# Dilated attention and a squared-ReLU FFN on one core: two more batches take the quadrant form of attention

## The chip, the cores and the metric

The kernel runs on one core of a Trainium2 chip. The metric is device time in microseconds: 310.31 us before, the median of three runs (309.73 to 311.42).

## The reference

Eight batches of eight heads, 576 tokens, head size 64. Heads 0 to 3 attend to the last 32 tokens (plain), heads 4 to 7 to every fourth of the last 128 (dilated). The attention output of all batches, 4608 tokens of 512 features, goes through a feed-forward network (FFN) with a squared ReLU.

```python
scores = scale * np.matmul(q, k.transpose(0, 1, 3, 2))
rel = pos[:, None] - pos[None, :]
mask_plain = (rel >= 0) & (rel < window)                              # window = 32
mask_dil = (rel >= 0) & (rel < window * dilation) & (rel % dilation == 0)   # dilation = 4
attn = np.exp(scores - max); attn = attn / np.sum(attn)
out = np.matmul(attn, v)                      # (8, 8, 576, 64)
x = out.transpose(0, 2, 1, 3).reshape(4608, 512)
h = np.maximum(x @ w_in, 0.0)                 # 512 -> 2048
return h * h @ w_out                          # 2048 -> 512
```

## The kernel before

**The order of the work is written by hand.** The FFN is cut into 288 groups, g0 to g287, mostly of four matmuls of 512 columns: for a tile of 512 tokens 16 groups of the first layer (L880, `mm1`, each followed by a ReLU on ACT, L893, and a square on DVE, L894) and 16 of the second (L922, `g2`; every fourth is followed by a copy to `osb` on ACT and a store). The first two tiles are done in halves of 256 tokens, 16 groups each (g0 to g63); g64 begins the tile of tokens 1024 to 1535, g96 the next. Each tile needs the attention output `xT` of its tokens: g48 to g51 those of batch 1's end, g64 to g67 those of batch 2, g96 those of batches 2 and 3. In g48 to g51 and g64 to g67 the first three heads' features come first (`cut = 3`) and the fourth head's two groups later. Attention is put between the groups: `PROGRAM` lists, divided by `|`, the steps that follow each group, and a list `steps` adds those of the quadrant form at a group number. Every engine carries out its instructions in the order in which they are issued here, and waits at the first one whose inputs or buffers aren't ready.

**PSUM.** Four buffers `pf` (FFN accumulators; also the spare pair of a step with an `f`), two `pa`, one `po`, one `pd`.

**The old form** (batches 1 to 3; batch 0 has one of its own). Heads go in pairs e = 0 to 3 (0, 1 plain, 2, 3 dilated; order 0, 2, 1, 3). Steps of `PROGRAM`, as `2k0` = batch 2, step k, pair 0: `q`, `k` make the transposed queries and keys, by transposes on TensorE (`trans`, L241) or from the crossbar buffer `xx` that a transposing DMA filled (`cross`), and copy them with `halves` (L261 to L278) into `qT` and `kbd`, where keys stand block by block, the two heads of a pair on the diagonal of a 128x128 block, zeros beside them. `v` spreads values likewise (`spread_v`, L212). `a`, `b` compute the scores of a pair's first and second half (`scores`, L317, L323, then Exp on ACT, L327, and the mask on DVE, L328; batch 3 also adds overlapping columns into `pm`, L337). `o`, `p` multiply by the values and sum (`pv`, L427, L429), take the reciprocal by Ln and Exp (L431, L432) and write `xT` (L442). A half is one step, so the eight halves of a batch take turns on two `pa` buffers.

**The quadrant form** (batches 4 to 7; `NATURAL = 4`). Queries and keys of all heads come from `xx` (for batch 2, XB, only the dilated heads are crossed; `xx[b % 2]` is the buffer). `arrange`: K, eight DVE copies of the plain heads' keys (L499), Q, four (L496), R, four small ones for the dilated heads' remainders (L504, L507). Then `quadrants` issues matmuls on 64x64 quarters of the array: S the scores of a pair into a pair of `pa` tiles, B first the values and sums of the pair before (into `po`, `pd` and the last 64 columns of the new `pa` tiles) and then the scores of the next, P values alone. E0 and E1 are Exp (L656) and mask (L658) of the two `pa` tiles; L four logarithms (L637, L638), X the exponential (L642) and three products into `xT` (L645, L647). A bundle B takes both `pa`, `po` and `pd`, so it needs E of its own scores and X of the values before. Bundles stand eight groups apart, L at the group of the bundle, X one later, E two and three later.

**Loads.** POOL issues the loads of q, k and v in the order of `PROGRAM`; v for the old form goes by `load_v` into blocks, for the quadrant form by `load_v_rows` into rows. SP issues the stores and the transposing DMAs.

Of the kernel before, what the change touches and what calls it, by code (L numbers as in the profile page):

```python
# [12 lines left out]
RES = 4  # L13
# [14 lines left out]
    "1o0 1o1f | 1a3 1Q0 | 1K0 1o3 | 1Q1 1K1 | 1Q2 | 1b0 | | 1Q3 1K2 L2:vwpdr L3:q00123 L3:q10123 | L2:x | | 2q0 | "  # L28
    "| 2k0 1V2 | 1b2 1p0 | 1b1 1V3 1K3 | | 1p2 1p1f | 2a0 1b3 | 2k1l 2b0 2o0 1p3f 2k1h | 2q1 2k2 L3:x | | 2q2 2p0 "
    "L3:vwpdr 2a1 | | | 2b1 | 2o1 2a2 2v2 2q3 | | 2p1f | 2k3 | 2b2 2o2 | 2v3 | 2a3 2p2f L4:q10123 | 2b3 2o3 | 3k1 "  # L30
    "| 2p3 | 3q1v L4:q00123 | 3k0l | | 3a1 3k0h | | 3k2l | 3o1 3q0a | 3k2h | | | 3a0 | 3b1 | 3q2 | | 3p1 L4:x "
    "L4:V | 3v2 | 3b0 | 3a2 3q3l 3o0 3q3h 3k3 | | | 3o2 3b2 | | 3p0 3v3 | 3a3 | 3p2 | L5:q10123 3b3 | 3o3 | | | "
    "L5:q00123 3p3 L5:V | | | | | | | | | | | | L5:x | | | | L6:q00123 | | | | | | | | | | | | | L6:q10123"
# [28 lines left out]
def kernel(  # L62
# [33 lines left out]
    ADDED = 3  # L96
    NATURAL = 4
# [7 lines left out]
    pm_pool = ctx.enter_context(tc.tile_pool(name="pm", bufs=4))  # L105
# [120 lines left out]
    def trans(b: int, e: int, nm: str, part: int, home: str):  # L226
# [4 lines left out]
        copy = copier(nm, e, home, True)  # L231
        if b == 2:
            m0, n, pitch, cuts = 0, M, M, [(t[0:80, a, :, :], MS[a], 80) for a in range(2)]
        else:

            m0, n, pitch, cuts = MS[part], MN[part], 80, [(t[0:80, part, :, :], 0, 80)]
# [7 lines left out]
        ready[b, e, nm] = pv_[:, :, :, 0:n], m0, n, copy  # L244
        halves(e, nm, *ready[b, e, nm], (0,) if "l" in home else (0, 1))
# [3 lines left out]
    def copier(nm: str, e: int, home: str, early: bool):  # L249
        act = "a" in home or "v" not in home and nm == "q" and e < NE // 2 and early  # L250
        return nc.scalar.copy if act else nc.vector.tensor_copy
# [31 lines left out]
    def blocks(b: int, e: int, part: int):  # L283

        if e < NE // 2:
            if b >= ADDED:
                return [(i, None, 16 * i, min(16 * i + 24, M)) for i in (range(4, NB) if part else range(4))]
            if part == 0:  # L290
                return [(i, None, 16 * i, min(16 * i + 24, 64)) for i in range(4)]
            return [(3, None, 64, 72)] + [(i, None, 16 * i, min(16 * i + 24, M)) for i in range(4, NB)]
        if b not in PARTED:
            rs = (2 * part, 2 * part + 1)
            return [x for r in rs for x in ((r, r, 0, 96), (4 + r, r, 64, M))] + [(8, None, 128, M)] * (part == 0)
        if part == 0:
            return [(r, r, 0, 64) for r in range(RES)]
        return [x for r in range(RES) for x in ((r, r, 64, 96), (4 + r, r, 64, M))] + [(8, None, 128, M)]

    def half_at(b: int, e: int):  # L300

        if e < NE // 2:
            return (384, mask_p[:, 384:832]) if b >= ADDED else (352, mask_p)
        return (256, mask_d) if b in PARTED else (416, mask_h)

    pts, pms = {}, {}

    def scores(b: int, e: int, part: int):
# [5 lines left out]
        for i, r, m0, m1 in blocks(b, e, part):  # L314
# [10 lines left out]
        off, mask = half_at(b, e)  # L325
# [4 lines left out]
            in1=mask[:, off : off + n] if b < ADDED and mask is not mask_h else mask[:, 0:n], op=ALU.mult,  # L330
        )
        if b < ADDED:
            return
        pm = pms[e, part] = pm_pool.tile([P, 160], bf16, name="pm")

        def add(to, x, y):
            nc.vector.tensor_tensor(out=to, in0=x, in1=y, op=ALU.add)  # L337

        if e >= NE // 2:
            main = pt[:, off : off + 352].rearrange("p (r c) -> p r c", r=2)  # L340
            add(pm[:, 0:64].rearrange("p (r m) -> p r m", r=2), main[:, :, 64:96], main[:, :, 96:128])
            return
        i0, n = (3, 4) if part else (0, 3)
        v = pt[:, 96 * i0 : 96 * (i0 + n + 1)].rearrange("p (i r m) -> p i r m", r=RES, m=24)
        add(
            pm[:, 0 : 32 * n].rearrange("p (i r m) -> p i r m", r=RES, m=8),
            v[:, 0:n, :, 16:24], v[:, 1 : n + 1, :, 0:8],
        )
        if part:
            add(  # L350
                pm[:, 128:160].rearrange("p (r m) -> p r m", r=RES), v[:, n, :, 16:24],
                pt[:, 768:832].rearrange("p (r m) -> p r m", r=RES)[:, :, 0:8],
            )

    def pv(b: int, e: int, part: int, spare=None, name=""):
# [8 lines left out]
        c = half_at(b, e)[0] * part  # L364
        byr = dil and b not in PARTED
        mms, dms = [], []
        if byr:
            n = 2 * M
            o3 = o[:, 0:n].rearrange("p (r m) -> p r m", r=2)
            d3 = d[:, 0:n].rearrange("p (r m) -> p r m", r=2)  # L370
            main = pt[:, c : c + 352].rearrange("p (r c) -> p r c", r=2)
            rem = pt[:, 352 + 32 * part : 384 + 32 * part].rearrange("p (r m) -> p r m", r=2)
            for x in range(2):
                mms.append((o3[:, x, 0:96], 2 * part + x, main[:, x, 0:96]))
                mms.append((o3[:, x, 64:M], 4 + 2 * part + x, main[:, x, 96:176]))
            mms.append((o3[:, :, 128:M], 8, rem))
            if b >= ADDED:
                pm = pms[e, part][:, 0:64].rearrange("p (r m) -> p r m", r=2)
                dms += [(d3[:, :, 0:64], main[:, :, 0:64]), (d3[:, :, 64:96], pm), (d3[:, :, 96:M], main[:, :, 128:176])]
            else:  # L380
                dms += [(d3[:, :, 0:96], main[:, :, 0:96]), (d3[:, :, 64:M], main[:, :, 96:176])]
            dms.append((d3[:, :, 128:M], rem))
        else:
            n = RES * MN[part]
            o3 = o[:, 0:n].rearrange("p (r m) -> p r m", r=RES)
            d3 = d[:, 0:n].rearrange("p (r m) -> p r m", r=RES)
            if not dil and b >= ADDED:

                i0 = 4 * part
                p4 = pt[:, 96 * i0 : 96 * i0 + 384].rearrange("p (i r m) -> p r i m", r=RES, m=24)  # L390
                d4 = d3.rearrange("p r (i m) -> p r i m", m=16)
                pm = pms[e, part]
                if part == 0:
                    dms.append((d4[:, :, 1:4, 8:16], p4[:, :, 1:4, 8:16]))
                    dms.append((d4[:, :, 1:4, 0:8], pm[:, 0:96].rearrange("p (i r m) -> p r i m", r=RES, m=8)))
                    dms.append((d4[:, :, 0, :], p4[:, :, 0, 0:16]))
                else:
                    dms.append((d4[:, :, 0:4, 8:16], p4[:, :, :, 8:16]))
                    b3 = pt[:, 288:384].rearrange("p (r m) -> p r m", r=RES)
                    b8 = pt[:, 768:832].rearrange("p (r m) -> p r m", r=RES)  # L400
                    dms.append((d4[:, :, :, 0:8], pm[:, 0:160].rearrange("p (i r m) -> p r i m", r=RES, m=8)))
                    dms.append((d4[:, :, 4, 8:16], b8[:, :, 8:16]))
                    mms.append((o3[:, :, 0:8], 3, b3[:, :, 16:24]))
                    mms.append((o3[:, :, 64:80], 8, b8))
                for i in range(4):
                    m1 = min(16 * i + 24, 64) if part == 0 else 16 * i + 24
                    mms.append((o3[:, :, 16 * i : m1], i0 + i, p4[:, :, i, 0 : m1 - 16 * i]))
            elif dil and part == 0:
                dms.append((d[:, 0:n], pt[:, 0:n]))
            elif dil:  # L410
                main = pt[:, c : c + 448].rearrange("p (r c) -> p r c", r=RES)
                rem = pt[:, c + 448 : c + 512].rearrange("p (r m) -> p r m", r=RES)
                dms += [(d3, main[:, :, 32:112]), (d3[:, :, 0:32], main[:, :, 0:32]), (d3[:, :, 64:80], rem)]
            for i, r, m0, m1 in () if mms else blocks(b, e, part):
                x0, x1 = m0 - MS[part], m1 - MS[part]
                if r is None:
                    w = RES * (m1 - m0)
                    rh = pt[:, c : c + w].rearrange("p (r m) -> p r m", r=RES)
                    mms.append((o3[:, :, x0:x1], i, rh))
                    if not dil:  # L420
                        dms.append((d3[:, :, x0:x1], rh))
                else:
                    w = m1 - m0
                    mms.append((o3[:, r, x0:x1], i, pt[:, c : c + w]))
                c += w
# [7 lines left out]
        t0 = b * S % RING  # L433
        tok = xT[:, e, t0 : t0 + S]
        if byr:
# [678 lines left out]
```

## Time and profile before

| | |
|---|---|
| time, median of three runs | 310.31 us (309.73 to 311.42) |
| profiled execution | 308.71 us, its span 306.8 us |
| TensorE (PE) busy | 295.2 us, 96% of the span, 2870 matmuls in the records |
| VectorE (DVE), ScalarE (ACT), GpSimd (POOL) busy | 177.7, 203.4, 96.1 us |
| granted TensorE clock | 0.999 |
| chain that ended last | PE 86%, DVE 6%, ACT 4% |
| FFN first layer, second layer on PE (L880, L922) | 130.4, 128.6 us busy |
| HBM read, written | 36.90 MB, 9.44 MB |

A group of instructions is named by the line of the kernel that issues it. A timeline's row has start, length, engine, line, operation, output and inputs, shapes, how many instructions were merged (x8), and in brackets the idle time of the engine before it and what ended it. Lengths of merged rows hold one latency at their end, so the pace is taken from starts.

### The profile page before, as it was taken

What the parts mean: (1) busy time and instruction counts of PE and PEld (TensorE: products, weight loads), DVE (VectorE), ACT (ScalarE), POOL (GpSimd) and SP (SyncE); (2) the same over time, 40 slices, a digit from 0 to 9 for tenths busy, and PEclk for the clock granted to TensorE, in tenths of its full rate; (3) what the DMA queues carried; (4) which work ended last, traced back from release to release, by engine and by line L of the source; (5) the groups of instructions that cost most, each with busy time, mean ns of one, the idle gap of its engine ahead of it and who ended that gap; (6) DMA issues with size and microseconds to landing.
All of it is one profiled execution on the core that took longest, in us unless ns stands there. A gap on an engine that the chain in (4) does not pass through costs nothing.

```text
span 306.8 us, 7297 instructions
## 1 busy us (share of the span) xinstructions
PE 295.2 (96%) x2870; PEld 172.3 (56%) x2903; DVE 177.7 (58%) x517; ACT 203.4 (66%) x439; POOL 96.1 (31%) x138
## 2 busy tenths in 40 slices
PE   8899999999999978999999999999999999999995
PEld 3599658769655544554455445544554445445543
DVE  1675567988988995468456855676563234104400
ACT  6888478869869744786579657865786576226511
POOL 8599683893065056230161208000000000000000
PEclk9999999999999999999999999999999999999999
DMA  8999999999979969998299869902200210121022
GB/s 115 196 180 214 204 162 224 174 150 185 154 111 196 157 100 204 139 148 131 69 133 152 103 142 103 164 16 65 61 2 13 68 61 0 35 71 34 0 64 75
DMA packets 80290, 35.09 MB, mean 114 GB/s; under 512 B 49920, under 2 KB 75648, under 8 KB 80256
## 3 DMA queue, kind: packets, MB, share of 16 engines
q0 software_dynamic: 46592, 18.23, 52.6%
q1 hardware_dynamic: 32976, 16.06, 26.0%
q8 instruction: 23, 0.38, 0.5%
q10 hardware_dynamic: 688, 0.33, 0.5%
q14 instruction: 11, 0.09, 0.1%
HBM read 36.90 MB, written 9.44 MB: 151 GB/s over the span
## 4 chain that ended last, share of the span: by engine, by line
PE 86%; DVE 6%; ACT 4%; issue 2%; ACTq 0%
PE pf L922 37%; PE pf L880 36%; PE po L674 2%; PE pa L529 2%; ACT h2T L893 2%; PE pd L529 1%; PE pa L241 1%; DVE h2T L894 1%; PE po L529 1%; PE po L427 1%; PE pa L704 1%; PE pd L429 1%; DVE kbd L499 1%; PE pf L756 1%; PE pa L323 1%
## 5 line engine op out<-in xcount | busy, mean ns | idle before, releaser
L880 PE MATMUL pf<-xT,w_in 128*128 128x512 bf16 (+1 forms) x693 | 130.4, 340 | 0.8
L922 PE MATMUL pf<-w_out_sb,h2T 128*128 128x512 bf16 (+2 forms) x570 | 128.6, 373 | 2.1 <-issue 1.4
L880 PEld LDWEIGHTS <-w_in 128*128 128x128 bf16 x704 | 76.9, 114 | 44.6 <-issue 1.1
L893 ACT ACTIVATE h2T<-pf 128x512 bf16<-128x512 f32 x144 | 82.4, 605 | 17.5 <-PE pf L880 17.0
L894 DVE TENSOR_TENSOR h2T<-h2T 128x512 bf16<-128x512 bf16 x144 | 60.1, 425 | 57.3 <-ACT h2T L893 53.0
L922 PEld LDWEIGHTS <-h2T 128*128 128x128 bf16 x592 | 54.7, 98 | 58.6
L928 ACT COPY osb<-pf 128x512 f32<-128x512 f32 (+1 forms) x36 | 20.7, 576 | 40.5 <-PE pf L922 37.6
L166 POOL DMA_DIRECT2D qb<-in_q_dram x18 | 13.6, 757 | 44.0 <-DMA xx<-qb 32.4
L645 DVE TENSOR_TENSOR xT<-po,rec 128x512 bf16<-128x512 f32 x16 | 11.1, 692 | 23.3 <-ACT rec L642 22.1
L656 ACT ACTIVATE pt<-pa 128x448 bf16<-128x448 f32 (+3 forms) x32 | 16.3, 509 | 9.3 <-DVE xT L647 9.3
L475 POOL DMA_DIRECT2D vd<-in_v_dram x16 | 9.9, 634 | 28.3 <-PE pa L529 24.8
L638 ACT ACTIVATE rec<-pd 64x512 f32<-64x512 f32 x32 | 18.6, 580 | 0.0
L183 POOL DMA_DIRECT2D vbd<-in_v_dram x20 | 13.9, 708 | 8.3 <-DMA kb<-in_k_dram 2.3
L327 ACT ACTIVATE pt<-pa 128x352 bf16<-128x352 f32 (+6 forms) x24 | 11.9, 506 | 4.1 <-PE pa L317 2.9
L431 ACT ACTIVATE rec<-pd 128x256 f32<-128x256 f32 (+2 forms) x19 | 7.8, 410 | 10.1 <-PE pd L429 10.1
L166 POOL DMA_DIRECT2D kb<-in_k_dram x18 | 13.6, 758 | 0.8 <-DMA vbd<-in_v_dram 0.4
L637 ACT ACTIVATE rec<-pa 64x64 f32<-64x64 f32 x32 | 7.0, 219 | 10.1 <-PE pa L529 9.5
L499 DVE COPY kbd<-xx 64x320 bf16<-64x320 bf16 (+1 forms) x32 | 13.0, 508 | 0.4
L484 POOL DMA_DIRECT2D vbd<-in_v_dram x16 | 12.5, 798 | 0.4 <-DMA qb<-in_q_dram 0.4
L442 DVE TENSOR_TENSOR xT<-po,rec 128x256 bf16<-128x256 f32 (+2 forms) x19 | 8.6, 454 | 6.5 <-ACT rec L432 5.7
L432 ACT ACTIVATE rec<-rec 128x256 f32<-128x256 f32 (+2 forms) x24 | 10.6, 443 | 0.8
L642 ACT ACTIVATE rec<-rec 128x576 f32<-128x576 f32 x16 | 10.9, 680 | 0.3
(128 smaller groups left out, 308.2 us busy)
## 6 DMA issues: line engine op xcount, KB each, us to landing
qb<-in_q_dram POOLq DMA_DIRECT2D x7, 320.0 KB, 5.4
kb<-in_k_dram POOLq DMA_DIRECT2D x7, 320.0 KB, 7.0
vd<-in_v_dram POOLq DMA_DIRECT2D x32, 64.0 KB, 6.2
w_in<-in_moe_w_in_dram POOLq DMA_DIRECT2D x4, 512.0 KB, 7.1
w_out_sb<-in_moe_w_out_dram POOLq DMA_DIRECT2D x4, 512.0 KB, 12.8
out_dram<-osb SPq DMA_DIRECT2D x16, 128.0 KB, 4.1
qb<-in_q_dram POOLq DMA_DIRECT2D x7, 256.0 KB, 7.2
kb<-in_k_dram POOLq DMA_DIRECT2D x7, 256.0 KB, 8.2
```

What stands on the lines that cost most here:

```text
L166: nc.gpsimd.dma_start(t[0:n, part, hs, :], src[b, hs, t0 : t0 + RES * n, :].rearrange("h (p r) d -> p h (r d)", r=RES))
L183: nc.gpsimd.dma_start(dst[rows, e, i0:i1, rows], v[b, 2 * e + hl, 64 * i0 : 64 * i1, :].rearrange("(i p) d -> p i d", p=64),)
L484: nc.gpsimd.dma_start(v_rows[b % 2][rows, e, :, :], v[b, 2 * e + hl, :, :].rearrange("(i p) d -> p i d", p=64))
L499: nc.vector.tensor_copy(k_both[rows, :, :].rearrange("p h (i m c j) -> p j c h i m", c=2, j=2, m=16)[:, jj, c, :, g::2, :], kx[b % 2][src, ...
L529: nc.tensor.matmul(out[sides[c]], lhs, rhs, start=begin, stop=True, skip_group_check=True)
L638: nc.scalar.activation(rec[to, 0:512], d[at, :], ACT.Ln)
L656: nc.scalar.activation(pt, sp[b, e][g][:, 0:n], ACT.Exp, scale=SCALE)
L880: nc.tensor.matmul(to, w_in_sb[piece][:, kt, c0 : c0 + 509 : 4], rhs, start=(kt == kts[0] and x == 0), stop=(kt == kts[-1] and x == per - ...
L893: nc.scalar.activation(hv, acc[u][:, :].rearrange("p (x n) -> p x n", x=per), ACT.Relu)
L894: nc.vector.tensor_tensor(out=hv, in0=hv, in1=hv, op=ALU.mult)
L922: nc.tensor.matmul(cur[m][:, c0:c1], h2[:, f, P * m : P * m + P], w_out_sb[:, f, c0:c1], start=(f == 0), stop=(f == NF - 1),)
L928: (nc.vector.tensor_copy if last and part == 1 else nc.scalar.copy)(osb[:, c0:c1], cur[m][:, c0:c1])
```

## The change

Batches 2 and 3 take the quadrant form too (`NATURAL = 2`), and the old form stays for batches 0 and 1 alone; its branches for other batches go (the additions `pm`, the dilated halves by residue, the layout of `xT` by halves). Batch 2's plain heads are still transposed on TensorE, since only its dilated heads are crossed, but each transposed pair is now copied whole into the crossbar buffer, q by ACT and k by DVE. v of batches 2 and 3 is loaded in rows. The 32 steps of each of the two batches leave `PROGRAM`, and bundles come at groups 50, 53, 56, 59 (batch 2, the last values at 62), 69, 75, 81, 86 (batch 3) and 91, 99, 107, 115 (batch 4, one earlier than before); E follows one group behind a bundle where the next is less than four away. K, Q and R copies of batches 2, 3 and 4 have group numbers of their own. In the code after, the bundles' matmuls are L448, K, Q, R L418, L415, L423 and L426, E L575 and L577, L L556 and L557, X L561 to L566, the whole copies L241, `xT` of the old form L366.

```diff
     PARTED = (0, 1)
-    ADDED = 3
-    NATURAL = 4
+    NATURAL = 2
...
-    pm_pool = ctx.enter_context(tc.tile_pool(name="pm", bufs=4))
...
# trans
-        copy = copier(nm, e, home, True)
-        if b == 2:
+        if b == XB:
             m0, n, pitch, cuts = 0, M, M, [(t[0:80, a, :, :], MS[a], 80) for a in range(2)]
...
-        ready[b, e, nm] = pv_[:, :, :, 0:n], m0, n, copy
-        halves(e, nm, *ready[b, e, nm], (0,) if "l" in home else (0, 1))
+        if b == XB:
+            copy = nc.scalar.copy if "a" in home else nc.vector.tensor_copy
+            copy((qx if nm == "q" else kx)[b % 2][:, 2 * e : 2 * e + 2, :, :], pv_)
+        else:
+            copy = copier(nm, e, home)
+            ready[b, e, nm] = pv_[:, :, :, 0:n], m0, n, copy
+            halves(e, nm, *ready[b, e, nm], (0,) if "l" in home else (0, 1))
...
# step
-        if what in "qk" and (b > XB or b == XB and e >= NE // 2):
-            t = (qx if what == "q" else kx)[b % 2]
-            halves(e, what, t[:, 2 * e : 2 * e + 2, :, :], 0, M, copier(what, e, home, b < ADDED), his)
...
# PROGRAM, from g36 on
-"| 1Q3 1K2 L2:vwpdr L3:q00123 L3:q10123 | L2:x | | 2q0 | "
-"| 2k0 1V2 | 1b2 1p0 | 1b1 1V3 1K3 | | 1p2 1p1f | 2a0 1b3 | 2k1l 2b0 2o0 1p3f 2k1h | 2q1 2k2 L3:x | | 2q2 2p0 "
-"L3:vwpdr 2a1 | | | 2b1 | 2o1 2a2 2v2 2q3 | | 2p1f | 2k3 | 2b2 2o2 | 2v3 | 2a3 2p2f L4:q10123 | 2b3 2o3 | 3k1 "
-"| 2p3 | 3q1v L4:q00123 | 3k0l | | 3a1 3k0h | | 3k2l | 3o1 3q0a | 3k2h | | | 3a0 | 3b1 | 3q2 | | 3p1 L4:x "
-"L4:V | 3v2 | 3b0 | 3a2 3q3l 3o0 3q3h 3k3 | | | 3o2 3b2 | | 3p0 3v3 | 3a3 | 3p2 | L5:q10123 3b3 | 3o3 | | | "
-"L5:q00123 3p3 L5:V | ...
+"| 1Q3 1K2 L2:V L3:q00123 L3:q10123 | L2:x | | 2q0a | | "
+"1V2 2k0 | 1b2 1p0 | 1b1 1V3 1K3 | 2q1a | 1p2 1p1f 2k1 | 1b3 | 1p3f | L3:x | | L3:V | | | | | | | | | | "
+"L4:q10123 | | | | L4:q00123 | | | | | | | | | | | | | | L4:x L4:V | | | | | | | | | | | L5:q10123 | | | | "
+"L5:q00123 L5:V | ...
...
# the quadrant form's steps
-    START = {NATURAL: (-10, -9, -3, -2, -1)}
+    BUNDLES = {2: (50, 53, 56, 59), 3: (69, 75, 81, 86), 4: (91, 99, 107, 115)}
+    COPIES = {2: (46, 46, 47, 48, 49), 3: (64, 65, 66, 67, 68), 4: (82, 83, 85, 86, 88)}
     for b in range(NATURAL, B):
-        base = G * (b - 1) - 4
-        for y, codes in zip(START.get(b, (-12, -10, -8, -6, -3)), COPIES):
-            steps += [(base + y + x, b, code) for x, code in enumerate(codes.split())]
-        for x, e in enumerate(ORDER):
-            at = base + 8 * x
-            steps.append((at, b, f"{'S' if b == NATURAL and x == 0 else 'B'}{e}"))
-            steps += [(at + 2, b, f"E{e}0"), (at + 3, b, f"E{e}1"), (at + 8, b, f"L{e}"), (at + 9, b, f"X{e}")]
+        ats = BUNDLES.get(b, tuple(G * (b - 1) - 4 + 8 * x for x in range(NE)))
+        for y, codes in zip(
+            COPIES.get(b, [ats[0] - z for z in (12, 10, 8, 6, 3)]), ("K00 K01", "K10 K11", "Q00 Q01", "Q10 Q11", "R00 R01")
+        ):
+            steps += [(y, 0, b, code) for code in codes.split()]
+        after = 62 if b == 2 else BUNDLES.get(b + 1, (G * b - 4,))[0]
+        for x, (e, at, to) in enumerate(zip(ORDER, ats, ats[1:] + (after,))):
+            steps.append((at, 1, b, f"{'B' if x or b > 3 else 'S'}{e}"))
+            y = 1 if to - at < 4 else 2
+            steps += [(at + y, 2, b, f"E{e}0"), (at + y + (y > 1), 2, b, f"E{e}1")]
+            steps += [(to, 3, b, f"L{e}"), (to + 1, 0, b, f"X{e}")]
+        if b == 2 or b == B - 1:
+            steps.append((after, 1, b, f"P{ORDER[-1]}"))
...
```

## The prediction

> **What bounds the kernel now.** I read the page's table of busy time first, then busy time by stretches of 10 us, then the chain that ended last, and then each engine's timeline around the stage that the change rewrites.
>
> ```profile
> PE 295.2 (96%) x2870; PEld 172.3 (56%) x2903; DVE 177.7 (58%) x517; ACT 203.4 (66%) x439; POOL 96.1 (31%) x138
> ```
>
> TensorE is busy for 96% of the span, so a time is the matmul work plus the moments when PE waits. The stretches (sum, then PE, PEld, DVE, ACT, POOL, granted clock, DMA) show where it waits:
>
> ```profile
> 100.00:110.00 10.00, 9.95 (x78) 5.50 (x79) 9.51 (x39) 7.05 (x16) 0.20 (x1) 1.00 1.11 143
> 110.00:120.00 10.00, 7.14 (x63) 3.83 (x61) 7.94 (x22) 4.59 (x10) 8.45 (x11) 1.00 1.05 146
> ```
>
> Nearly all of PE's idle time lies in 110 to 120, behind a VectorE that was full (9.51 of 10) just before. That is batch 3 in the old form with batch 4's copies in DVE's queue. PE's timeline names the waits:
>
> ```profile
> 112.20 0.39 PE L427 MATMUL po<-pt,vbd 128*128 128x32 bf16 x6 [1.97 <-DVE xT L442]
> 119.15 0.23 PE L529 MATMUL pa<-qT,kbd 64*64 64x96 bf16 x2 [0.21 <-DVE qT L496]
> 120.16 0.36 PE L529 MATMUL pa<-qT,kbd 64*64 64x96 bf16 x16 [0.79 <-DVE qT L496]
> ```
>
> With a gap of 0.16 after them these are 3.1 us. The chain, late in the kernel, gives the pace of the FFN:
>
> ```profile
> 289.34 10.14 PE pf L922 x47
> ```
>
> 10.14/47 is 0.216 us a matmul, so 0.86 us for a group of four, wherever PE is not kept waiting. Now one bundle of the new form, on PE, where batches 4 to 7 use it already:
>
> ```profile
> 127.80 0.36 PE L529 MATMUL po<-pt,vbd 64*64 64x96 bf16 x8
> 128.20 0.34 PE L529 MATMUL pa<-xx 64*64 64x96 bf16 x16
> 128.50 7.10 PE L880 MATMUL pf<-xT,w_in 128*128 128x512 bf16 x31
> ```
>
> Values and sums take 0.40, scores 0.30, a bundle 0.70 (0.77 where its values are dilated: 135.53 to 136.30). What follows it on ACT and DVE, from the bundle whose next FFN group begins at about 151.85:
>
> ```profile
> 151.99 0.22 ACT L637 ACTIVATE rec<-pa 64x64 f32<-64x64 f32 x1 [1.11 <-PE pa L529]
> 153.43 0.68 ACT L642 ACTIVATE rec<-rec 128x576 f32<-128x576 f32 x1
> 155.00 0.54 ACT L656 ACTIVATE pt<-pa 128x448 bf16<-128x448 f32 x1 [0.88 <-DVE xT L647]
> ```
>
> ```profile
> 141.63 3.30 DVE L499 COPY kbd<-xx 64x320 bf16<-64x320 bf16 x8
> 144.97 0.94 DVE L496 COPY qT<-xx 64x1152 bf16<-64x1152 bf16 x2
> 154.15 0.69 DVE L645 TENSOR_TENSOR xT<-po,rec 128x512 bf16<-128x512 f32 x1 [3.74 <-ACT rec L642]
> 154.76 0.47 DVE L647 TENSOR_TENSOR xT<-pa,rec 64x64 bf16<-64x64 f32 x2
> 155.57 0.39 DVE L658 TENSOR_TENSOR pt<-pt,mask_p 128x448 bf16<-128x448 bf16 x1 [0.35 <-ACT pt L656]
> ```
>
> This is a round that nothing shortens: four logarithms (1.44), the exponential (0.72 to the next start), the products into xT (0.85 to the first L647), the exponential of the new scores, which waits for that L647 because scores and tails share a PSUM tile, and the mask. From the FFN group after a bundle to the first mask's end: 0.14 + (155.96 - 151.99) = 4.1 us; the second half's mask ends about 0.4 later. The next bundle multiplies those very scores, so it begins effectively 4.4 us after the last one. At today's spacing of eight groups PE has 6.9 us of FFN in between and never notices.
>
> **The change, part by part.** Groups are numbered g as in the text above; before, g48 begins at 69.8, g54 at 76.2, g64 at 87.8, g70 at 93.2 and g96 at 123.4.
>
> *PE work removed.* The old form's pieces in the PE timeline add up to 4.4 us for batch 2 and 4.1 for batch 3 (sixteen pieces each of 0.15 to 0.45). The new form is 2 x 0.70 + 2 x 0.77 = 2.9 a batch. Saved: 8.5 - 5.8 = 2.7. With the 3.1 of waits that go with batch 3's old form: -5.8 us. Bounds: -4.5 (part of the waits return) to -6.3. Batch 2's 32 transposes stay (0.28 for eight).
> [...]
>
> *Evacuation of batch 2's transposes.* Eight copies a pair (four of 0.50 on DVE for k, 0.40 on ACT for q) become one of 576 columns; the nearest row is a 640-column copy, 0.49 on DVE, 0.69 on ACT. About 1.5 us less on DVE and 0.9 on ACT a head pair, but the L499 and L496 copies come instead: 3.3 for K, 1.9 for Q (four of 0.47), 0.85 for R, on DVE alone.
>
> *g46 to g53: copies ahead of batch 1's last product.* DVE's order now has the eight K copies ahead of xT of step 1p3f, and u3 of g49 (its PSUM buffer) and g50 (its tokens) wait for that. Walking the queues from the old timeline: PE reaches 1p3f at 69.1 and waits for its mask until 69.9 (0.8); g48 begins at 70.4; DVE makes K from 69.9 to 73.2, xT to 73.7, Q to 75.6. u3 could start at 72.4: 1.4 lost. Scores S0 after g50 could start at 74.85, Q ends 75.6: 0.8. The bundle at g53 waits 0.4 for exponentials behind four relus (0.49 each). Together 3.4 us; less 0.4 of work no longer there, g54 begins at 79.2, 3.0 late. Bounds 2.0 to 4.5.
>
> *g53 to g66: batch 2's rounds.* Bundles stand at 50, 53, 56, 59, the last values at 62: only three groups, 2.6 us, between them. Each wait is 4.4 - 2.6 = 1.8; the first round also has a relu (0.5) in ACT's queue between logarithm and exponential: 2.35, 1.75, 1.85, sum 5.95. Bounds 4.5 (first halves enough: 1.5 each) to 7.0 (0.35 more each). PE reaches g64 at 95.8, 7.9 late. The last product of batch 2 (xT of head 3) ends 3.9 after P3, and g66 needs it after 3.45: 0.45.
>
> *g64 to g69: batch 3's copies.* They stand behind that product on DVE: K 3.3, two squares 0.7, Q 0.94, two squares 0.7, Q 0.94, so S0 can begin 3.9 + 6.6 = 10.5 us after P3. PE has g63 to g69, 6.05 us, plus the 0.45: 10.5 - 6.5 = 4.0 us of waiting. Bounds 2.5 to 5. g70 begins at 105.8, 12.5 late. Before, this stretch held no wait of PE.
>
> *g70 to g96.* Spacings 6, 6, 5, 5. At g81 the round just fits (0.15, relus included). At g86 DVE's order puts batch 4's eight K copies (3.3) ahead of the masks of E10 and E11: products end 3.4 after g81's bundle, K at 6.7, masks 7.1 to 7.4; five groups are 4.3: 2.8 lost. At g91 batch 4's R copies stand ahead of the masks: 0.9. Together 3.85, bounds 1.5 to 5. g96 begins at 135.1.
>
> *At no cost.* POOL issues as many V loads for batches 2 and 3 as before (ten each); batch 4's must now wait for P3 at 95 instead of going out at 89.9, take some 10 us as then, and are needed at g99, near 138. The crossbar transposes on SP keep their places; batch 4's end at 105.7 and its K copies start at 120. If these covers went, S0's row (4 us) would be the size of the loss. From g99 on only a group's shift is left.
>
> *Sum.* -5.8 + 3.4 + 5.95 + 0.45 + 4.05 + 3.85 = +11.9; the walk, group by group, gives 135.1 - 123.4 = +11.7, which I take. The profiled execution took 308.71 (span 306.8), so 320.4; the median of the three runs, 310.31, stands 1.6 higher, so 322.0.
>
> The longest wait is 4 us, and PE's clock was granted at 1.00 through the 2.9 idle us of 110 to 120. [...]
>
> **The rivals.**
> - *Batch 3's copies stay hidden.* If PE's waits in batch 2 let DVE run ahead, the waits at g69, g86 and g91 vanish (4.05 + 2.8 + 0.9): 322.0 - 7.75 = 314.3. For it: DVE is idle in those waits. Against: its queue is in order, and K of batch 3 stands behind the last product of batch 2, which ends the last round.
> - *The waits cost more than themselves.* Each of the two longest slows what follows, by a gap as long as the widest one seen (1.97): +3.9, 326. For it: squares and relus bunch up behind copies. Against: 110 to 120 shows no such slowing.
> - *Faster.* The rounds hide and only the savings stay: 310.3 - 5.8 = 304.5. It decides if a round is under 3.4 us (three groups and a bundle). For it: batches 4 to 7 show no wait. Against: they have eight groups, and the rows give 4.4 plus the bundle.
> - That the new form isn't used is out: its quadrant matmuls stand at these groups in the changed kernel's order.
>
> **How the numbers follow.** Forecast 0.72, first rival 0.13, second 0.08, faster 0.05, no change 0.02 (all errors cancel). The terms' bounds sum to 2.0 + 4.5 + 0 + 2.5 + 1.5 - 6.3 = +4.2 and 4.5 + 7.0 + 0.5 + 5 + 5 - 4.5 = +17.5, that is 314.5 to 327.8; with the first rival's end the range is 314 to 327.5. It leaves out the faster case, no change, and the tails. The three runs before spread by 0.5%, about what a measurement can tell from no change; slower by more: 0.93, within: 0.02, faster: 0.05.
>
> **What would show it.** Right: PE waits of 1.5 to 2.4 us before the bundles at g56, g59 and g62, released by the masks of L577 (L658 before); about 4 us before S0 of batch 3, released by the Q copies; about 1.4 inside g49, released by xT of L366; 2 to 3 at g86 behind K copies; a first 512-column FFN matmul near 96 instead of 87.8. Wrong: bundles less than 4 us apart on PE, E starting before the L566 product ends, or K copies running while batch 2's last logarithms do.

## The result and the profile after

326.11 us, the median of four runs (324.85 to 326.28), against 310.20 for the kernel before in the same comparison (309.73 to 311.42): a ratio of 1.0498, 95% interval 1.0458 to 1.0538. The profiled execution took 326.12, its span 324.2. The range (314 to 327.5) holds it and the sign is right; the number of the likeliest case, 322.0, is 4.1 too low. Executions of one and the same kernel differ in their mean granted clock: of the 17 of the kernel before beside the run e9_gapfit, ten with 0.998 or more have a median of 309.27, seven with 0.992 to 0.994 one of 311.84, so a difference of 1 us between kernels is read from the traces too.

The page of the kernel after, its table of busy time:

```profile
PE 299.9 (93%) x3078; PEld 170.9 (53%) x3113; DVE 171.2 (53%) x473; ACT 204.6 (63%) x437; POOL 95.4 (29%) x138
```

PE's share fell from 96% to 93%, and its busy time grew by 4.7 although two batches were to need less of it. I cut the span at the first matmul of g32 and of g96, between which nearly all of the change lies. Busy time between them, first before, then after (stretch; its length; PE, PEld, DVE, ACT, POOL; granted clock; DMA):

```profile
50.38:123.39 73.01, 69.39 (x680) 47.18 (x688) 63.06 (x212) 53.16 (x121) 36.52 (x54) 1.00 1.34 161
```
```profile
52.23:141.07 88.84, 74.47 (x887) 45.92 (x897) 57.22 (x167) 54.08 (x119) 34.45 (x51) 0.92 0.98 129
```

The stage takes 88.84 instead of 73.01, +15.83. PE's idle time went from 3.62 to 14.37 (+10.75), its busy time from 69.39 to 74.47 (+5.08), and the clock from 1.00 to 0.92. What is left of the 17.41 between the two profiled executions is 1.85 of start-up (g32 at 52.23 instead of 50.38, with a longer wait for `w_in`; profiles of kernels with the same start have it between 50.38 and 52.23) and -0.27 after g96.

PE's timeline after, its waits in order: the old form's last step, its `xT`, S0 of batch 2, the bundles at g53 and g56, P at g62, S0 of batch 3 twice, the bundle at g86:

```profile
71.28 0.43 PE L359 MATMUL pf<-pt,vbd 128*128 128x32 bf16 x9 [0.34 <-DVE pt L321]
75.06 1.25 PE L799 MATMUL pf<-xT,w_in 128*128 128x256 bf16 x10 [1.15 <-DVE xT L366]
76.88 0.36 PE L448 MATMUL pa<-qT,kbd 64*64 64x96 bf16 x16 [0.41 <-DVE qT L415]
79.93 0.35 PE L448 MATMUL pd<-pt,mk 64*64 64x384 bf16 x2 [0.39 <-DVE pt L577]
85.36 0.27 PE L448 MATMUL pd<-pt,mk 64*64 64x192 bf16 x2 [1.83 <-DVE pt L577]
95.94 0.27 PE L448 MATMUL pd<-pt,mk 64*64 64x192 bf16 x2 [1.45 <-DVE pt L577]
105.99 0.23 PE L448 MATMUL pa<-qT,kbd 64*64 64x96 bf16 x2 [2.35 <-DVE qT L415]
107.76 0.53 PE L448 MATMUL pa<-qT,kbd 64*64 64x96 bf16 x16 [1.54 <-DVE qT L415]
129.99 0.35 PE L448 MATMUL pd<-pt,mk 64*64 64x384 bf16 x2 [2.65 <-DVE pt L577]
```

The releasers are those that the prediction named: masks (L577) before bundles, Q copies (L415) before S0, `xT` of L366 inside g49. DVE's timeline shows the K copies (L418) ahead of what PE waits for, at two of the three places:

```profile
71.15 3.33 DVE L418 COPY kbd<-xx 64x320 bf16<-64x320 bf16 x8
74.51 0.49 DVE L366 TENSOR_TENSOR xT<-pf,rec 128x320 bf16<-128x320 f32 x1
...
126.23 3.28 DVE L418 COPY kbd<-xx 64x320 bf16<-64x320 bf16 x8
129.54 0.66 DVE L577 TENSOR_TENSOR pt<-pt,mask_p 128x448 bf16<-128x448 bf16 x2
```

What the prediction's sum did not have is in the granted clock (the column after POOL's), in these four stretches of the kernel after:

```profile
85.00:90.00 5.00, 4.26 (x67) 2.33 (x69) 2.04 (x6) 3.00 (x8) 2.82 (x4) 0.66 0.46 53
105.00:110.00 5.00, 2.47 (x23) 1.14 (x23) 4.15 (x13) 0.00 (x0) 0.00 (x0) 0.65 1.45 206
110.00:115.00 5.00, 4.78 (x16) 2.04 (x16) 1.98 (x5) 3.10 (x6) 2.81 (x4) 0.67 0.49 57
130.00:135.00 5.00, 4.67 (x60) 2.50 (x62) 2.72 (x7) 2.57 (x6) 0.00 (x0) 0.66 0.11 43
```

In them the clock is 0.50 from 85.99 to 89.40, from 106.47 to 113.29 and from 130.36 to 133.77. Each follows a wait: 1.83 before g56's bundle, 2.35 and 1.54 around S0, 2.65 at g86. The matmuls of 512 columns then start 0.43 us apart, not 0.216. In the profiled execution before, the clock was 1.00 through the whole stage.

### The profile page after: what moved, and what is told of

Read it like the earlier page. It is cut to its first block, busy times and chain, and to the rows that moved or that the text cites. A ratio compares the mean times of both kernels' runs of the same rounds, so it can differ in the third digit from the quotient of the medians.

```text
span 324.2 us, 7631 instructions
## 1 busy us (share of the span) xinstructions
PE 299.9 (93%) x3078; PEld 170.9 (53%) x3113; DVE 171.2 (53%) x473; ACT 204.6 (63%) x437; POOL 95.4 (29%) x138
## 4 chain that ended last, share of the span: by engine, by line
PE 77%; DVE 7%; DMA 7%; ACT 4%; issue 3%; POOL 1%; ACTq 0%; POOLq 0%
PE pf L841 35%; PE pf L799 35%; DVE kbd L418 3%; DMA w_in<-in_moe_w_in_dram 3%; PE pa L448 2%; DMA qb<-in_q_dram 2%; PE pd L448 2%; DMA out_dram<-osb 2%; PE po L448 1%; ACT rec L557 1%; DVE qT L415 1%; PE pa L236 1%; DVE h2T L813 1%; ACT rec L561 1%; ACT rec L556 0%
## 5 line engine op out<-in xcount | busy, mean ns | idle before, releaser
L564 DVE TENSOR_TENSOR xT<-po,rec 128x512 bf16<-128x512 f32 x24 | 16.6, 691 | 42.5 <-ACT rec L561 41.0
L575 ACT ACTIVATE pt<-pa 128x448 bf16<-128x448 f32 (+3 forms) x48 | 23.5, 507 | 14.5 <-DVE xT L566 14.5
L557 ACT ACTIVATE rec<-pd 64x512 f32<-64x512 f32 x48 | 27.8, 579 | 0.0
L556 ACT ACTIVATE rec<-pa 64x64 f32<-64x64 f32 x48 | 10.5, 219 | 17.9 <-PE pa L448 17.1
L448 PEld LDWEIGHTS <-mk 64*64 64x64 bf16 x288 | 11.0, 106 | 17.0 <-issue 8.4
L418 DVE COPY kbd<-xx 64x320 bf16<-64x320 bf16 (+1 forms) x48 | 19.6, 508 | 0.6
L403 POOL DMA_DIRECT2D vbd<-in_v_dram x24 | 18.7, 802 | 1.4 <-issue 1.4
L448 PE MATMUL pd<-pt,mk 64*64 64x192 bf16 (+4 forms) x168 | 12.5, 253 | 6.5 <-DVE pt L577 6.3
L561 ACT ACTIVATE rec<-rec 128x576 f32<-128x576 f32 x24 | 16.3, 680 | 0.4
L415 DVE COPY qT<-xx 64x1152 bf16<-64x1152 bf16 x24 | 10.9, 454 | 0.7
L566 DVE TENSOR_TENSOR xT<-pa,rec 64x64 bf16<-64x64 f32 x48 | 10.4, 217 | 0.8
L577 DVE TENSOR_TENSOR pt<-pt,mask_p 128x448 bf16<-128x448 bf16 (+1 forms) x24 | 8.8, 373 | 3.2 <-ACT pt L575 3.2
```

The lines of the kernel that those rows point to most:

```text
L403: nc.gpsimd.dma_start(v_rows[b % 2][rows, e, :, :], v[b, 2 * e + hl, :, :].rearrange("(i p) d -> p i d", p=64))
L418: nc.vector.tensor_copy(k_both[rows, :, :].rearrange("p h (i m c j) -> p j c h i m", c=2, j=2, m=16)[:, jj, c, :, g::2, :], kx[b % 2][src, ...
L448: nc.tensor.matmul(out[sides[c]], lhs, rhs, start=begin, stop=True, skip_group_check=True)
L557: nc.scalar.activation(rec[to, 0:512], d[at, :], ACT.Ln)
L561: nc.scalar.activation(rec[:, :], rec[:, :], ACT.Exp, scale=-1.0)
L575: nc.scalar.activation(pt, sp[b, e][g][:, 0:n], ACT.Exp, scale=SCALE)
```

## The experiments

Theory A: the loss is PE's waits, at the prediction's places, plus the half-clock stretches that they bring on. "Stage" below is the time from g32 to g96 of the profiled execution.

| kernel | median us | ratio to before (95%) | stage | PE busy | PE idle | clock in the stage |
|---|---|---|---|---|---|---|
| before | | | 73.01 | 69.39 | 3.62 | 1.00 |
| after | 326.11 | 1.0498 (1.0458 to 1.0538) | 88.84 | 74.47 | 14.37 | 0.92 |
| e1_fill | 321.74 | 1.0335 (1.0284 to 1.0386) | 85.50 | 77.82 | 7.68 | 1.00 |
| e2_k3 | 322.07 | 1.0332 (1.0260 to 1.0404) | 86.06 | 73.28 | 12.78 | 0.94 |
| e3_k4 | 322.05 | 1.0372 (1.0319 to 1.0426) | 87.61 | 74.57 | 13.04 | 0.92 |
| e4_round | 322.00 | 1.0329 (1.0264 to 1.0393) | 84.21 | 71.75 | 12.46 | 0.96 |
| e6_order | 315.30 | 1.0154 (1.0106 to 1.0202) | 78.61 | 69.46 | 9.15 | 1.00 |
| e5_b3 | 311.46 | 1.0000 (0.9974 to 1.0025) | 75.09 | 70.06 | 5.03 | 0.98 |
| e7_b3order | 308.99 | 0.9955 (0.9921 to 0.9989) | 73.65 | 69.26 | 4.39 | 1.00 |
| e8_even | 315.47 | 1.0156 (1.0110 to 1.0202) | 78.65 | 71.27 | 7.38 | 0.96 |
| e9_gapfit | 308.99 | 0.9955 (0.9919 to 0.9990) | 71.45 | 69.16 | 2.29 | 1.00 |

### Keeping the clock up: e1_fill

```diff
+    FILL = {(2, "B1"): 7, (2, "B3"): 5, (2, "P3"): 6, (3, "S0"): 10, (3, "B3"): 11}
+    def fill(n: int):
+        to = ps_f.tile([P, NT], f32, name="pf")
+        rhs = idle[:, :].unsqueeze(1).broadcast_to([P, 2, 256])
+        for _ in range(n):
+            nc.tensor.matmul(to[:, :], idle[:, 0:P], rhs, start=True, stop=True)
     def natural_step(b: int, code: str):
+        if (b, code) in FILL:
+            fill(FILL[b, code])
```

> Theory A: about 4 of the 15.8 us that the changed kernel loses by g96 are TensorE running at half its clock after waits (granted clock 0.50 to 0.68 in three stretches, at 86 to 90, 106 to 114 and 130 to 134 us). Here PE multiplies zeros into an unused PSUM tile in front of the five longest waits (7, 5, 6, 10 and 11 products of 512 columns, 0.216 us each at full clock), so that it doesn't idle there; nothing else is changed and the products are used nowhere. A expects a granted clock of 1.00 in all these stretches, and a time 3 to 4 us below the changed kernel: 322 to 323. Rival B: the half clock only fills time that the next round's wait would have taken anyway. It expects the clock back at 1.00 and the time unchanged, 325.5 to 326.5, with longer waits behind. Rival C: the slow stretches have nothing to do with idling; the clock still drops with the products there, and the time is unchanged or, with products run at half clock, 1 to 3 us longer.

321.74, and the same four stretches:

```profile
85.00:90.00 5.00, 4.53 (x77) 2.25 (x69) 2.00 (x6) 3.50 (x8) 2.82 (x4) 1.00 0.34 40
105.00:110.00 5.00, 3.44 (x30) 1.96 (x31) 4.00 (x13) 1.84 (x4) 0.00 (x0) 1.00 1.30 158
110.00:115.00 5.00, 4.95 (x69) 2.73 (x68) 2.24 (x6) 4.37 (x11) 2.83 (x4) 1.00 0.71 81
130.00:135.00 5.00, 4.06 (x73) 2.13 (x73) 2.29 (x9) 3.01 (x8) 1.65 (x3) 1.00 0.35 109
```

The clock stays at 1.00 and the stage is 3.34 shorter: A; B and C are out. A part of B is true. At full clock the bundle at g59 waits for its masks again (0.32, after 5 products or 1.08), and so does the one at g91 (0.78); in the kernel after the slow matmuls in front of them had used that time up. That is why 5 us of extra PE busy time cost 3.3.

### The round of batch 2: e4_round

```diff
+            if b == 2:
+                nc.scalar.activation(rec[:, 512:576], d[:, 448:512], ACT.Ln)
+                nc.scalar.activation(rec[:, 0:512], d[:, :], ACT.Ln)
-            for g in range(2):
+            for g in range(2) if b > 2 else ():
```

> Batch 2's logarithms are two ScalarE operations of 128 partitions (the tail's taken from the wrong columns, and the halves not swapped, so the output for batch 2 is not the reference's) instead of four of 64: about 0.75 us instead of 1.44 in each round. Theory A: the round of 4.4 us after each bundle sets the spacing of batch 2's bundles, so each of three rounds shrinks by about 0.65; the waits of 1.83 at g56 and 1.45 at g62 fall to about 1.2 and 0.8, and with shorter waits the first half-clock stretch may go: 322.5 to 324.5. Rival: VectorE, not the round, sets the spacing (products and masks queue behind squares): waits and time unchanged, 325.5 to 326.5.

322.00, slightly better than A's bounds. The wait at g56 is 1.33 and that at g62 0.40 (1.83 and 1.45 after; expected 1.2 and 0.8), and no half-clock stretch follows the first (1.00 from 85 to 90). ScalarE's four logarithms are thus on the path of each round; VectorE alone doesn't set it. (With two logarithms for four, this kernel's output for batch 2 is not the reference's.)

### The copies ahead of S0 and of the masks: e2_k3, e3_k4

e2 moves batch 3's K copies ahead of batch 2's last product, e3 batch 4's K copies behind the masks:

```diff
-    COPIES = {2: (46, 46, 47, 48, 49), 3: (64, 65, 66, 67, 68), 4: (82, 83, 85, 86, 88)}
+    COPIES = {2: (46, 46, 47, 48, 49), 3: (61, 61, 66, 67, 68), 4: (82, 83, 85, 86, 88)}   # e2_k3
+    COPIES = {2: (46, 46, 47, 48, 49), 3: (64, 65, 66, 67, 68), 4: (85, 85, 86, 87, 93)}   # e3_k4
```

> Batch 3's eight K copies (3.3 us of VectorE) are issued after g61, ahead of batch 2's last product, instead of after g64 and g65. Theory A: they then run while VectorE waits for batch 2's last logarithms; the wait before S0 of batch 3 (2.35 and 1.54 us in the changed kernel) falls to about 0.6 or less and the half-clock stretch behind it goes (2.5 us): 320 to 321. Rival: VectorE has no room there, the last product of batch 2 comes 1 to 3 us later and g66 waits for it instead, so the time stays at 324 to 326.

> The changed kernel with batch 4's eight K copies (3.3 us) issued after g85, behind the masks of batch 3's third head instead of ahead of them, and its R copies after g93. Theory A: between the bundles at g81 and g91 VectorE has about as much to do as there is time, so the 2.65 at g86 goes but K, the products, Q and the last masks end late for g91: a wait of about 1.5 there (0 in the changed kernel), so about 1 us less of waiting, and another 1 to 1.7 if the wait is too short for a half-clock stretch: 323.5 to 325.5. Rival: the order alone makes the wait; both waits are under 0.5 and the time falls by the whole of 2.65 and 1.7, to about 322.

e2: 322.07, that is 4.0 below the kernel after, where A expected 5 to 6 and the rival 2 at most. PE's timeline around S0 of batch 3:

```profile
102.79 0.23 PE L448 MATMUL pa<-qT,kbd 64*64 64x96 bf16 x2 [0.33 <-DVE qT L415]
104.56 0.38 PE L448 MATMUL pa<-qT,kbd 64*64 64x96 bf16 x16 [1.54 <-DVE qT L415]
```

The first wait fell from 2.35 to 0.33, as K's time came free; the second stayed at 1.54, because the last two Q copies follow squares of the groups just ahead of S0 and not K. A half-clock stretch still follows (0.68 in 105 to 110).

e3: the trace agrees with A, the wait at g86 is gone and one at g91 takes its place:

```profile
134.13 0.27 PE L448 MATMUL pd<-pt,mk 64*64 64x192 bf16 x2 [1.57 <-DVE pt L577]
```

1.57 (expected 1.5) instead of 2.65, no half clock behind it (1.00 from 130 to 140), and a stage shorter by 1.23, although PE turns slow after the old form's `xT` inside g49 (a wait of 1.43 there; 20 matmuls of 256 columns from 76.44 on take 3.75, in e6_order 2.37). The median, 322.05, is below A's 323.5 to 325.5; the profiled execution took 323.67. Moving K within this window moves the wait: 3.3 of K, 1.9 of Q, two sets of products and masks do not fit between g81 and g91.

### Room for the copies: e6_order

K and Q belong to pairs 0 and 1 alone, so with the pairs in the order 0, 1, 2, 3 they can be overwritten a bundle earlier (in the texts on record "heads" means these pairs):

```diff
-ORDER = (0, 2, 1, 3)
+ORDER = (0, 1, 2, 3)
...
-    COPIES = {2: (46, 46, 47, 48, 49), 3: (64, 65, 66, 67, 68), 4: (82, 83, 85, 86, 88)}
+    COPIES = {2: (46, 46, 47, 48, 49), 3: (56, 59, 62, 63, 70), 4: (78, 79, 84, 85, 93)}
...
-            steps += [(y, 0, b, code) for code in codes.split()]
+            steps += [(y, 0 if b == 2 or b > 4 else 4, b, code) for code in codes.split()]
```

> The changed kernel with the heads of batches 2 to 7 in the order 0, 1, 2, 3 instead of 0, 2, 1, 3. K and Q are used by heads 0 and 1 alone, so the next batch's copies need not wait for a batch's third bundle: batch 3's K now follows the bundles at g56 and g59, its Q g62 and g63, batch 4's K g78 and g79, its Q g84 and g85, R after the first bundle. Theory A: batch 2's rounds and the waits up to g62 stay, the waits before S0 (3.9) and at g86 (2.65) and the half-clock stretches behind them (4 together) go, with up to 1 us of new waits: 315 to 318. Rival: the copies, wherever they stand, delay batch 2's products by as much as they save at S0: 320 or more.

315.30, as A said. The bundles of the rounds:

```profile
83.91 0.35 PE L448 MATMUL pd<-pt,mk 64*64 64x384 bf16 x2 [1.86 <-DVE pt L577]
88.94 0.27 PE L448 MATMUL pd<-pt,mk 64*64 64x192 bf16 x2 [1.39 <-DVE pt L577]
94.14 0.27 PE L448 MATMUL pd<-pt,mk 64*64 64x192 bf16 x2 [1.39 <-DVE pt L577]
```

No wait at S0 of batch 3, 0.35 at g86, no half clock (1.00 from 80 to 140). The rounds stay, 4.64 us, and with the 2.1 around g46 to g50 they are most of the 9.15 that is left. The stage's PE time (see the table) holds a second answer. At full clock PE is busy for 69.46 us with the quadrant form of both batches, against 69.39 before: placed like this, the new form saves nothing.

The reason is that a bundle has no single length. From its first product to the FFN's next one, the bundle at g75, with its masks ready and a first-layer group behind it, takes 0.71 us, as the prediction had it. The one at g81, ahead of a second-layer group, takes 0.94. Those that began as soon as the first half's mask was there take 0.90 to 1.28, because they wait inside for the second half's; some 0.2 us of it count as busy time (the row at 88.94 begins such a bundle). All in all these pieces take 9.4 us in the stage, some 0.3 of it batch 4's first scores. The kernel before shows the second price too: each of its bundles takes 0.70 to 0.78 ahead of a first-layer group, and 0.93 to 1.00 ahead of a second-layer group, here from 143.33 to 144.26:

```profile
143.33 0.35 PE L529 MATMUL pd<-pt,mk 64*64 64x384 bf16 x2
144.26 1.03 PE L922 MATMUL pf<-w_out_sb,h2T 128*128 128x512 bf16 x4 [0.16 <-issue]
```

### Batch 3 alone: e5_b3, e7_b3order, e8_even, e9_gapfit

Batch 2 keeps the old form, so its rounds are gone. Against the kernel before (all steps of batch 3 leave `PROGRAM`, its v is loaded in rows):

```diff
-    NATURAL = 4
+    NATURAL = 3
...
+    BUNDLES = {3: (69, 75, 81, 86), 4: (91, 99, 107, 115)}                    # e5, e7
+    COPIES = {3: (62, 63, 65, 66, 68), 4: (82, 83, 85, 86, 88)}              # e5
+    ORDER = (0, 1, 2, 3)                                                      # e7, e8, e9
+    COPIES = {3: (62, 63, 65, 66, 71), 4: (78, 79, 84, 85, 93)}              # e7
+    BUNDLES 3: (67, 73, 79, 85); COPIES = {3: (60, 61, 63, 64, 69), 4: (76, 77, 82, 83, 93)}   # e8
+    BUNDLES 3: (71, 75, 81, 86); COPIES = {3: (62, 63, 65, 66, 72), 4: (80, 81, 86, 86, 91)}   # e9
```

> The kernel before, with batch 3 alone in quadrant form at the changed kernel's groups (69, 75, 81, 86; batch 4 from 91), and batch 2 in the old form; batch 3's K copies after g62 and g63, its Q copies after g65 and g66. Theory A: without batch 2's rounds 3 groups apart and the copies behind them, nothing is lost up to g70 but at most 0.5 us; saved are 4.1 - 2.9 = 1.2 of TensorE work and the 3.1 of waits; the 2.65 at g86 comes back, with a half-clock stretch of about 1.7 behind it: 310.2 - 4.3 + 4.4 = 310.3, between 308.5 and 312. Rival: batch 3's form is itself the loss (VectorE has no room for its copies between g62 and g91): 316 or more, with waits at g69 as in the changed kernel.

> The kernel before with batch 3 alone in quadrant form, as in the run e5_b3 (311.46), and the head order 0, 1, 2, 3, batch 4's K copies after g78 and g79, Q after g84 and g85, R of both batches after the first bundle. Theory A: the wait of 2.85 at g86 and the half-clock stretch behind it (about 1.5) go, the 0.9 at g69 stays: about 307, between 306 and 308.5, below the kernel before. Rival: the wait moves to g81 or g91 because VectorE is full there as in the kernel before: 310 to 312.

> As the run e7_b3order, with batch 3's bundles after g67, 73, 79 and 85, so that six groups lie between all of them, and batch 3's copies two groups earlier. Theory A: the rounds at g86 and g91, which five groups (4.3 us) fit only just, no longer wait, but the copies for S0 of batch 3 have no more room than before: within 1 us of e7_b3order, 306 to 308. Rival: VectorE is not done with batch 2's old form at g67; S0 waits 2 us or more: 309 or more.

> As the run e7_b3order (308.99; batch 3 alone in quadrant form, heads in the order 0, 1, 2, 3), with its three remaining waits of TensorE addressed one by one: S0 of batch 3 stands after g71 instead of g69 (1.02 before its scores there), batch 4's K copies after g80 and around the bundle of g81, by which time the crossing that they waited 1.85 for on VectorE has landed (1.86 of TensorE at g80), and its Q copies behind the bundle of g86, R behind that of g91. Theory A: copies that stand just behind a bundle run while ScalarE takes the logarithms and cost nothing: no wait over 0.5 between g60 and g96, 308.99 - 2.9 = 306, between 305.5 and 307.5. Rival: 3.3 us of K copies do not fit between g80 and the products at g82; masks come 1 us or more late at g86 and the time stays at 308 to 310.

e5: 311.46, within A's bounds, no difference from before. The wait at g86 came back as 2.85, half clock behind it (0.73 from 115 to 120); S0 waited 0.90. Batch 3's form is not the loss by itself.

e7: 308.99, above A's 306 to 308.5. The wait at g86 fell to 0.36, but a new one stands at g80:

```profile
111.98 2.98 PE L911 MATMUL pf<-w_out_sb,h2T 128*128 128x512 bf16 x13 [1.86 <-DVE h2T L883]
```
```profile
109.71 1.76 DVE L488 COPY kbd<-xx 64x320 bf16<-64x320 bf16 x4 [1.85 <-DMA xx<-kb]
111.50 0.43 DVE L883 TENSOR_TENSOR h2T<-h2T 128x512 bf16<-128x512 bf16 x1
```

DVE's queue stood still for the crossing that K reads, and a square behind K kept g80 waiting. Neither theory had named that transfer.

e8: 315.47, the rival's side, but for another reason. S0 waited 0.59 and the old form 0.87; the bundle at g85 waited 4.57. K of batch 4 is issued ahead of the crossing here (g76 against g78), so pairs 0 and 1 of batch 4 use keys that an earlier batch left in the buffer, and the crossing has to wait until they are read (it is issued at 109.49, in e7 at 101.47). Its Q, in DVE's queue:

```profile
119.26 1.91 DVE L485 COPY qT<-xx 64x1152 bf16<-64x1152 bf16 x4 [6.92 <-DMA xx<-qb]
```

So e8 says nothing about even spacing; it shows what a copy costs that is ordered on the wrong side of a transfer.

e9: 308.99 again, not A's 306. The copies do fit behind bundles; the longest wait from g64 to g96 is 0.66. The stage is 1.56 shorter than before, of which 1.33 is idle time and 0.23 PE's work. It is 2.20 shorter than e7's, where the expectation counted on 2.9, and yet the medians of the two are equal; e7's profiled execution, 310.78, lies 1.8 above its median, so its stage may not be its usual one. e9's profiled execution also began 1.6 later than the kernel before (g32 at 52.02) and took 308.73, against 308.71. e7 and e9 are the fastest kernels here, by 0.45%, about the 0.5% that a measurement can tell; a gain over the kernel before is not shown.

### Which waits bring the half clock: e10_gaps, e11_gaps2, e12_gaps3

```diff
+    GAPS = {145: 2, 153: 4, 177: 3, 185: 5, 209: 6, 217: 1, 242: 3, 250: 4, 274: 2, 281: 5}   # e10
+    scr = mask_d[:, 0:NT]
+    def gap(n: int):
+        to = ps_f.tile([P, NT], f32, name="pf")
+        rhs = idle[:, :].unsqueeze(1).broadcast_to([P, 2, 256])
+        nc.tensor.matmul(to[:, :], idle[:, 0:P], rhs, start=True, stop=True)
+        nc.vector.tensor_copy(scr[:, :], to[:, :])
+        for _ in range(n):
+            nc.vector.tensor_tensor(out=scr[:, :], in0=scr[:, :], in1=scr[:, :], op=ALU.max)
+        nc.tensor.matmul(to[:, :], idle[:, 0:P], scr[:, :], start=True, stop=True)
...
         group()
+        if g in GAPS:
+            gap(GAPS[g])
```

> The kernel before with ten made waits of TensorE, at g145, 153, 177, 185, 209, 217, 242, 250, 274 and 281: a product into an unused PSUM tile, a VectorE copy of it and 2, 4, 3, 5, 6, 1, 3, 4, 2 and 5 passes over the copy (about 0.38 each), and a product that reads the last of them, so waits of about 1.2 to 3.1 us (0.8 + 0.38 a pass). It asks which waits are followed by a half-clock stretch. Theory A, from the traces so far (1.83, 2.35 and 2.65 were followed by one, 1.97, 1.44 and less were not): waits of 2.3 us and over are followed by one of 3 to 6 us, those under 1.5 by none, and near 1.9 it goes either way. Rival: the length of the single wait doesn't decide, and long waits without and short ones with such a stretch are both seen.

> Made waits as in the run e10_gaps, where single waits of 1.44, 1.70, 2.16 and 2.62 us were followed by no half clock and those of 3.08 and over were. Here waits of about 2.1 us (1.0 + 0.42 a pass where VectorE is free) stand directly ahead of a bundle of quadrant products (g148, 164, 188, 212, 220) and, of the same size, with no bundle for four groups or more behind them (g200, 230, 242, 250, 274). [...] Rival: where the wait stands doesn't matter; waits of 2.1 to 2.6 are followed by none at either place, and any stretch follows a wait of 3 or more.

> As the run e11_gaps2, with the sizes turned round: about 1.7 us ahead of the bundles at g188, 212 and 220, 2.2 to 2.6 at g200, 230, 242, 250 and 274, away from bundles. Theory A: 1.7 ahead of a bundle is near the edge, as 1.83 was at g56 of the changed kernel, and one or two of the three are followed by a half-clock stretch; none of the five elsewhere is. Rival: none at all, or more of the long ones than of those ahead of bundles.

Two rows of e11, waits of one size, both directly ahead of a bundle (g188 and g212), the first followed by a stretch at 0.50, the second by none:

```profile
230.43 0.38 PE L631 MATMUL pf<-mask_d,kbd 128*128 128x512 bf16 x1 [2.16 <-DVE mask_d L630]
265.71 0.38 PE L631 MATMUL pf<-mask_d,kbd 128*128 128x512 bf16 x1 [2.16 <-DVE mask_d L630]
```

| made wait, us | directly ahead of a bundle: half clock after | elsewhere |
|---|---|---|
| 3.03 to 4.24 | 1 of 1 | 9 of 9 |
| 2.57 to 2.62 | 1 of 1 | 1 of 6 |
| 2.15, 2.16 | 1 of 3 | 0 of 3 |
| 1.44 to 1.70 | 0 of 3 | 0 of 2 |

The made waits of 3.03 or more were all followed by it (10 of 10), those of 1.70 or less never (0 of 5), and between them it went either way (3 of 13). Theory A fails in e10, where a wait of 2.62 brought none, and in e12, which fits its rival (none of its 1.7 ahead of a bundle, two of the longer ones elsewhere). e11 asked whether a wait brings it sooner directly ahead of a bundle: of the waits near 2.1 there one did and two did not, and elsewhere none of two; those of 2.57 did at both places, which speaks against the rival.

The granted clock in the traces shows more. In the kernel after, the half-clock stretches last 3.41, 6.83 and 3.41 us, and their starts (85.99, 106.47 and 130.36) lie 6 and 7 times 3.41 us apart. So the trace can be divided from such a moment on, forwards and backwards, into windows of 3.41 (in the kernel before, from the drop at its end, at 306.31), and PE's busy time counted in each. In the kernels before and after 179 whole windows ran at full clock. The four in which PE was busy for 1.48 us or less were each followed by half clock; the other 175, with 1.89 or more, never. In the kernel after, the stretch at 106.47 went on for a second window, with PE busy for 2.12 in its first; the windows that ended a stretch had 3.08, 3.08 and 3.19. The window that holds the wait at g56 in the kernel after (1.83), and the two windows over which the same wait of e6_order (1.86) is spread:

```profile
82.57:85.98 3.41, 1.48 (x36) 0.66 (x37) 2.37 (x7) 2.29 (x5) 0.00 (x0) 1.00 0.59 131
```
```profile
79.90:83.31 3.41, 2.09 (x15) 1.40 (x14) 1.46 (x4) 2.50 (x6) 0.00 (x0) 1.00 1.65 191
83.31:86.73 3.42, 2.66 (x56) 1.61 (x58) 2.82 (x7) 2.72 (x8) 0.02 (x1) 1.00 0.54 119
```

The two waits of 2.16 in e11 differ likewise: PE is busy for 1.25 in the window of the first, for about 2.1 and 2.4 in the two that share the second. So in these traces neither the length of a wait alone nor the bundle behind it parts those that were followed by half clock from the others, but how little PE did within one window: the wait of 1.83 lies within a window, that of 1.86 is spread over two. The wait of 1.97 in the kernel before is spread over two as well, with PE busy for 1.89 and 2.91, and no half clock follows.

## Why the prediction was right or wrong

- *The places.* Every wait that it named was found, with the releaser that it named, except those at g59, g81 and g91. g59's and g91's are there once the clock is kept up (1.39 in e6_order, 0.78 in e1_fill; forecast 1.75 and 0.9); g81's 0.15 was nothing.
- *Their sizes.* The terms add up to 17.7; PE's idle time after is 14.37, all small gaps included. g46 to g53: 2.29 for 3.4. The rounds: 4.64 at full clock for 5.95, within the bounds; they were computed until the second half's mask, and e6_order's 1.39 is what the lower bound ("first halves enough", 1.5) has. S0: 3.89 for 4.0. g86: 2.65 for 2.8. g66: 0.27 for 0.45.
- *PE work removed, 2.7: the step that failed by its own account.* It added the timeline's rows of the old pieces (8.5) and took a bundle at 0.70 to 0.77, from two bundles that stand ahead of first-layer groups and wait for nothing; the same trace had 0.93 and 1.00 ahead of second-layer groups. In e6_order, at full clock, the new pieces take about 9.1 (batch 4's 0.3 left out), not 5.8, and PE as a whole is busy for 69.46 against 69.39: saved is -0.07, and 0.23 where batch 3 alone is changed (e9_gapfit).
- *The clock, left out of the sum.* The sum rests on a clock of 1.00 through the 2.9 idle us of 110 to 120 and has no term for a slower one. The half clock added 5.0 of PE busy time and 3.34 of time (the stage, against e1_fill). The second rival, "the waits cost more than themselves", 326, was right in size; its reason (squares and relus bunching up) was not the one, and its "against" (110 to 120 shows no slowing) was one wait of 1.97 that happened to bring none. Waits of 1.83, 2.35 and 2.65 (after) and of 2.16 and 2.57 (e11_gaps2) were followed by half clock; in the windows ahead of the three stretches of the kernel after PE was still busy for 1.48, 0.82 and 0.77.
- *How the errors add up.* Forecast for the stage: -2.7 - 3.1 + 17.7 = +11.9, of which the walk made 11.7. Measured: PE's work +0.07, idle time +10.75, the clock +5.0, together +15.8. With the clock kept up (e1_fill) the stage is 12.5 longer than before, within 1 us of the forecast. That closeness is in part luck: waits forecast too long by 2.1 (14.6 net of those before, against 12.5 of idle time and zeros in e1_fill) nearly paid for the 2.7 of saving that wasn't there. The miss of 4.1 is the 3.3 that the half clock added to the stage and the 0.8 that is left (12.5 against 11.7).
- *At no cost:* POOL's loads and the crossings held nobody up in the kernel after. e7_b3order and e8_even show how near the crossing was: with K four groups earlier, at g78, it is late.

## What to carry to other kernels

A matmul saving worked out from the lengths of rows is no saving until PE's whole busy time over a stage shows it: what a bundle costs depends on what stands behind it and on whether its last input is there when it begins (0.78 to 1.28 here for the same products). Forecast waits of TensorE can cost more than themselves: here waits of 1.83 to 2.65 were followed by three half-clock stretches, 3.3 us together, and an order that removes it (here which pair frees the shared buffer first, 10.2 us of the stage) is worth more than shifting copies about. Put copies that nobody waits for directly behind a bundle, while another engine works on its result, and on the late side of the transfer that feeds them.

## What the runs showed of the hardware that was not expected

The granted clock dropped to 0.50 after waits of 1.83, 2.35 and 2.65 us (after), for 3.41 or 6.83 us at a time (the longest from 106.47 to 113.29), and the same wait in the same place brought it in one run and not in another: 1.83 at g56 of the kernel after did, 1.86 there in e6_order did not. In the kernels before and after it went with PE's busy time within windows of 3.41 us: 1.48 or less was followed by it four times of four, 1.89 or more in none of 175. Zeros multiplied into an unused PSUM tile kept the clock at 1.00 and made the stage 3.34 us shorter without changing any of its own work.
